# Whole-unit products, other Horner halves and a new step order in a fused attention and rational-activation kernel

## Chip, cores and metric

The kernel runs on one core of a Trainium2 chip. The metric is the device time of one execution in microseconds (us); the time given for a kernel is the median of its runs. An engine name in the text is as the profile has it: PE (TensorE), DVE (VectorE), ACT (ScalarE), POOL (GpSimd), SP (SyncE, which issues most transfers).

## What is computed

A linear attention with squared sketch features, followed by a two-layer network whose activation is a ratio of two polynomials. The core of the reference:

```python
# attention: q, k, v are (4, 4, 1088, 32), S1 and S2 are (8, 32)
def phi(x):
    a = np.einsum('rd,bhsd->bhsr', S1, x)
    b = np.einsum('rd,bhsd->bhsr', S2, x)
    return np.einsum('bhsi,bhsj->bhsij', a, b).reshape(*x.shape[:-1], r * r)
q_p, k_p = (phi(q), phi(k))
kv = np.einsum('bhsf,bhsd->bhfd', k_p, v)
z = np.sum(k_p, axis=2)
num = np.einsum('bhsf,bhfd->bhsd', q_p, kv)
den = np.einsum('bhsf,bhf->bhs', q_p, z)[..., None] + 1e-06
x = (num / den) as (4352, 128)          # tokens by heads * dims

# network: w_in (128, 2048), w_out (2048, 128), a (4,), b (2,)
h = x @ w_in
P = a[0] + a[1] * h + a[2] * h**2 + a[3] * h**3
Q = 1.0 + np.abs(b[0]) * np.abs(h) + np.abs(b[1]) * h**2
out = (P / (Q + 1e-06)) @ w_out
```

## The kernel before

**The order.** Nothing is scheduled by the framework: `ORDER` is a written list of some 700 steps, `name:index`, and the loop at the end of the kernel calls one function for each. The position in the list is the position in the in-order queue of the engine that the step uses. Loads (`lk`, `lq`, `lv` of a batch's K, Q, V; `lw`, `lx` of halves of w_out and w_in; `lq:0` of the rest of the first Q) go to SP's queue, in list order too, together with scratch transfers and stores.

**Attention.** Four batches. For each batch K is transposed on DVE (`kt`), sketched on PE (`ks`), copied on ACT (`kc`), multiplied out on DVE (`kf`), contracted with V on PE (`kp`) and kept by ACT (`kk`). Q goes in blocks of tokens (`:0` to `:12`): transposed (`qt`, DVE), sketched (`qs`, PE), copied (`qc`, ACT; from block 3 on through scratch memory in DRAM, by seven transfers on SP), multiplied (`qf`, DVE), contracted (`qp`, PE), divided (`qd` on ACT or DVE, `qi` and `qx` on DVE), transposed back (`qb`, PE) and copied to `xT` (`qk`, ACT). One SBUF buffer each serves all K and all Q loads, so a load waits for the transposes of the one ahead.

**The network.** The hidden layer is worked in 17 units of 4096 columns each: unit 0 has 256 tokens by all 16 blocks of 128 hidden rows, units 1 to 14 have 512 tokens by 8 blocks, units 15 and 16 have 256 tokens by 16 blocks. In each unit:

- `h0` to `h3` (L455, PE): a part of 1024 columns of h = x @ w_in into one of two PSUM tiles `h_ps`; `e0` to `e3` (L461, ACT) evict it to `hh` in bf16.
- `u` (L484, DVE): |h| by a bit mask; `w` (L490, DVE): |b1| u + |b0|; `y` (L495, DVE): w times u. So w holds Q − 1.
- `ln` (L546) and `ex` (L550, both ACT): r = exp(−ln(1 + 1e-6 + w)) = 1 / Q, always in halves of 2048 columns.
- `p` (`pd` L536 on DVE or `pa` L541 on ACT, by `P_ON_ACT`): a3 h + a2.
- `s` (L554, DVE): s = h r. `m` (L558, DVE): g = h s. `x` (L569, DVE): g = g p. So g = (a3 h + a2) h² r.
- `G0` to `G5` (L588, PE), one group for each half and each of r, s, g: out += r (a0 w_out) + s (a1 w_out) + g w_out, with the two scaled copies of w_out made once (`wo`, L621 to L625). `st` (L597, L605) transposes and stores.

In a **Horner half** (`HORNER` lists 2 × unit + half) m is h p, a step `v` (L564, DVE) adds a1, and x multiplies by s: g = h r (a1 + h (a2 + a3 h)). The s group of that half is then left out on PE.

A step's digit is the half (or quarter in unit 16). `u`, `w`, `y` work on the whole unit at digit 1 unless the unit is in `SPLIT_A`. `s`, `m`, `x`, `p` work in halves unless the unit is in `WIDE_S`, `WIDE_M`, `WIDE_X`, `WIDE_P` and, for m and x, both halves are of one Horner kind or, for p, on one engine; then the step of digit 0 does nothing and that of digit 1 does both halves. (By this rule only s of units 3 and 5 is whole before.) Unit 16 is always in half and quarters.

The buffers behind this: three of `hh`, one of `u`, two of `w`, one of `ln`, and rings of halves: four each of r, s and g, two of p:

```python
rings = {key: big.tile([128, n, HW], BF, name=key) for key, n in (("r", 4), ("s", 4), ("g", 4), ("p", 2))}
```

`tn` (L170) issues matmuls on zeros: `tn:0` eleven, `tn:4` two.

Of the kernel before, what the change touches and what calls it, by code (L numbers as in the profile page):

```python
# [26 lines left out]
ex0:0 u1:1 h2:2 qf:3 w1:1 qc:4 e1:2 qp:3 e2:2 s0:0 pa0:0 h3:2 y1:1 h0:2 qd:3 wo:5 e3:2 qi:3 m0:0 G0:0 e0:2 qx:3 G1:0
ln0:1 kt1:2 x0:0 qb:3 ks0:2 u1:2 qk:3 G2:0 ex0:1 lk:3 pd0:1 G3:0 w1:2 G4:0 pa1:1 kp1:1 y1:2 kc0:2 ln1:1 G5:0 qf:4 lv:2
qs:5 kf0:2 kk:1 ex1:1 qp:4 s0:1 ks1:2 qd:4 qc:5 qi:4 ln0:2 qt:7 G0:1 qx:4 m0:1 qb:4 G1:1 qk:4 s1:1 ex0:2 h3:3 x0:1
kc1:2 h2:3 m1:1 e3:3 kf1:2 h0:3 e2:3 kt1:3 ln1:2 s0:2 h1:3 st:0 m0:2 e0:3 qs:7 x1:1 e1:3 h2:4 ex1:2 u1:3 h3:4 pd1:2  # L30
pa0:2 w1:3 kp1:2 s1:2 e2:4 x0:2 e3:4 h0:4 lv:3 qf:5 pa0:3 y1:3 qp:5 qc:7 e0:4 h1:4 m1:2 qd:5 ln0:3 qi:5 qt:9 G2:1 qx:5
e1:4 x1:2 qb:5 G3:1 qk:5 u1:4 ex0:3 G4:1 m0:3 G5:1 pa1:3 G0:2 w1:4 h0:5 kt0:3 ln1:3 m1:3 h2:5 y1:4 kk:2 ex1:3 ks0:3
G1:2 e0:5 s1:3 G2:2 ln0:4 G3:2 h1:5 v0:3 ex0:4 qf:7 x0:3 G4:2 e2:5 qs:6 s0:4 qc:6 h3:5 e1:5 pd0:4 ln1:4 m0:4 h1:6 v1:3
e3:5 x0:4 pa1:4 h0:6 u1:5 qt:8 G5:2 e1:6 w1:5 ex1:4 h3:6 st:2 y1:5 e0:6 qp:7 e3:6 s1:4 G0:3 pa0:5 lq:3 G2:3 x1:3 qs:8
m1:4 h2:6 ln0:5 m0:5 G3:3 e2:6 x1:4 G5:3 ex0:5 qf:6 G0:4 u1:6 G1:4 qc:8 qd:7 ln1:5 qi:7 qp:6 w1:6 G2:4 qx:7 qd:6 pa0:6
qi:6 v0:5 qb:7 G3:4 qx:6 y1:6 qb:6 qk:7 G4:4 qk:6 ex1:5 h3:7 m0:6 pa1:5 G5:4 s1:5 h1:7 e3:7 st:4 h2:7 m1:5 e1:7 ln0:6
x0:5 h0:7 qt:10 x1:5 e2:7 G0:5 e0:7 qf:8 ks1:3 kc0:3 ex0:6 u1:7 qs:9 h1:8 v0:6 qc:9 w1:7 ln1:6 h3:8 s0:6 e1:8 pd1:6
qp:8 ex1:6 y1:7 h0:8 e3:8 s1:6 kc1:3 ln0:7 h2:8 x0:6 e0:8 m1:6 G2:5 qd:8 ex0:7 G3:5 qi:8 kf0:3 G4:5 kf1:3 G5:5 e2:8
qs:10 ln1:7 u1:8 kp1:3 qx:8 w1:8 ex1:7 qb:8 G0:6 qf:9 qk:8 y1:8 qc:10 h3:9 pa0:7 s0:7 h0:9 e3:9 s1:7 ln0:8 h2:9 qt:12
m0:7 e0:9 G0:7 x1:6 e2:9 h1:10 ex0:8 x0:7 qt:11 h1:9 u1:9 pa0:8 m1:7 G2:6 pd1:7 e1:9 G3:6 s0:8 e1:10 G4:6 u0:9 ln1:8  # L40
h3:10 w1:9 m0:8 qp:9 ex1:8 x1:7 h2:10 x0:8 qd:9 kk:3 e3:10 qi:9 w0:9 pa0:9 h0:10 qf:10 y0:9 qp:10 e2:10 y1:9 e0:10
# [676 lines left out]
```

## Time and profile before

| | |
|---|---|
| runs | 272.06, 272.32 and 272.9 us; median 272.32 |
| profiled execution | span 270.8 us from its first to its last instruction; the median of the runs is 1.5 us above that span |
| ACT | 248.8 us busy, 224 instructions |
| DVE | 256.7 us busy, 278 instructions |
| PE | 257.7 us busy, 1382 matmuls; weight loads 147.5 us |
| granted clock of PE | 0.994 in the mean |
| memory | 16.16 MB read, 3.15 MB written |

How to read the rows: in a timeline row stand start, duration, engine, line, operation, output and inputs, shape, and in brackets the idle time before it with what ended it. In a group row stand the count, busy time and mean duration in ns, then the idle time before its instructions. In a row of stretches stand, for each engine, busy us and the number of instructions. Neighbouring instructions of one engine overlap at their ends, so the step from one start to the next is shorter than the duration.

### The profile page before, as it was taken

The page shows a single profiled execution, that of the slowest core. Times are in us where ns is not written, and L with a number is a line of the kernel's source. Part 1 is how long each engine was busy: PE and PEld are TensorE (multiplying, and loading weights), DVE is VectorE, ACT ScalarE, POOL GpSimd, SP SyncE. Part 2 cuts the span into 40 slices and gives each one's busy share as a digit, 9 for nine tenths or more (in the row PEclk, how much of TensorE's full clock was granted, in tenths as well). Part 3 has the DMA queues.
Part 4 walks back from the last instruction along what each step waited for, and adds up shares of the span by engine and source line. Part 5 has one row for each costly group of instructions (what it writes and reads, how often), then busy time and mean ns, then how long its engine had stood idle before and what let it go on. Part 6 is the DMA issues. An engine that isn't in the chain of part 4 may idle for free.

```text
span 270.8 us, 3732 instructions
## 1 busy us (share of the span) xinstructions
PE 257.7 (95%) x1382; PEld 147.5 (54%) x1397; DVE 256.7 (95%) x278; ACT 248.8 (92%) x224; POOL 2.9 (1%) x24
## 2 busy tenths in 40 slices
...
DMA packets 30530, 19.55 MB, mean 72 GB/s; under 512 B 20400, under 2 KB 26672, under 8 KB 30512
## 3 DMA queue, kind: packets, MB, share of 16 engines
...
q8 instruction: 11, 0.18, 0.3%
...
HBM read 16.16 MB, written 3.15 MB: 71 GB/s over the span
## 4 chain that ended last, share of the span: by engine, by line
ACT 47%; PE 34%; issue 8%; DVE 5%; DMA 4%; SPq 0%; ACTq 0%; DVEq 0%
PE h_ps L455 16%; ACT ln L546 13%; ACT r L550 12%; ACT hh L461 12%; PE att_ps L588 10%; ACT p L541 7%; PE att_ps L365 3%; DMA v_sb<-in_v_dram 2%; PE att_ps L302 2%; DMA k_sb<-in_k_dram 2%; DVE g L558 2%; DVE s L554 1%; ACT xT L398 1%; PE att_ps L391 1%; PE att_ps L409 1%
## 5 line engine op out<-in xcount | busy, mean ns | idle before, releaser
L455 PE MATMUL h_ps<-xT,w_in_sb 128*128 128x512 f32 (+1 forms) x320 | 125.8, 537 | 2.8 <-ACT hh L461 1.9
L455 PEld LDWEIGHTS h_ps<-xT,w_in_sb 128*128 128x128 f32 x320 | 58.3, 190 | 55.2 <-issue 37.3
L461 ACT CAST hh<-h_ps 128x1024 bf16<-128x1024 f32 x68 | 67.5, 1027 | 3.5 <-PE h_ps L455 3.1
L588 PEld LDWEIGHTS <-w_out 128*128 128x128 bf16 x460 | 45.5, 100 | 45.9 <-issue 14.3
L546 ACT ACTIVATE ln<-w 128x2048 f32<-128x2048 bf16 (+1 forms) x35 | 66.0, 1887 | 0.7 <-DVE w L495 0.6
L550 ACT ACTIVATE r<-ln 128x2048 bf16<-128x2048 f32 (+1 forms) x35 | 65.8, 1880 | 0.6 <-PE att_ps L588 0.2
L541 ACT ACTIVATE p<-hh,a_sb 128x2048 bf16<-128x2048 bf16 (+1 forms) x23 | 46.7, 2035 | 0.1
L554 DVE TENSOR_TENSOR s<-hh,r 128x2048 bf16<-128x2048 bf16 (+2 forms) x33 | 41.0, 1246 | 0.2 <-ACT r L550 0.2
L495 DVE TENSOR_TENSOR w<-w,u 128x4096 bf16<-128x4096 bf16 (+2 forms) x22 | 39.4, 1798 | 0.1
L588 PE MATMUL att_ps<-g,w_out 128*128 128x512 bf16 (+1 forms) x154 | 34.8, 350 | 4.3 <-DVE g L569 3.9
L558 DVE TENSOR_TENSOR g<-hh,s 128x2048 bf16<-128x2048 bf16 (+1 forms) x30 | 35.2, 1175 | 0.0
L569 DVE TENSOR_TENSOR g<-g,p 128x2048 bf16<-128x2048 bf16 (+1 forms) x30 | 35.1, 1178 | 0.1
L588 PE MATMUL att_ps<-r,w_out 128*128 128x512 bf16 (+1 forms) x154 | 34.8, 353 | 0.3
L588 PE MATMUL att_ps<-s,w_out 128*128 128x512 bf16 (+1 forms) x137 | 29.3, 342 | 0.2
L490 DVE TENSOR_SCALAR w<-u,b_abs 128x4096 bf16<-128x4096 bf16 (+2 forms) x22 | 23.8, 1090 | 0.0
L484 DVE TENSOR_SCALAR u<-hh 128x4096 uint16<-128x4096 uint16 (+2 forms) x22 | 21.4, 976 | 1.6 <-ACT hh L461 1.5
L365 PEld LDWEIGHTS att_ps<-kvz,q_pT 128*128 128x128 f32 x144 | 17.7, 191 | 4.6 <-issue 2.0
L365 PE MATMUL att_ps<-kvz,q_pT 128*128 128x66 f32 x144 | 17.9, 273 | 0.1
L302 PEld LDWEIGHTS att_ps<-v_sb,k_p 128*64 128x64 f32 (+1 forms) x288 | 8.8, 138 | 1.9 <-DVE qT L325 0.8
L536 DVE TENSOR_SCALAR p<-hh,a_sb 128x2048 bf16<-128x2048 bf16 x12 | 9.7, 808 | 0.0
L302 PE MATMUL att_ps<-v_sb,k_p 128*64 128x64 f32 (+1 forms) x288 | 9.2, 223 | 0.5 <-DMA v_sb<-in_v_dram 0.5
L273 DVE TENSOR_TENSOR k_p<-att_ps,b_sk 128x1024 f32<-128x1024 f32 (+2 forms) x8 | 9.3, 1178 | 0.1
...
## 6 DMA issues: line engine op xcount, KB each, us to landing
...
k_sb<-in_k_dram SPq DMA_DIRECT2D x3, 544.0 KB
q_sb<-in_q_dram SPq DMA_DIRECT2D x3, 544.0 KB
...
w_out_sb_f<-in_moe_w_out_dram SPq DMA_DIRECT2D x2, 512.0 KB
```

The costliest lines, as they stand in the source:

```text
L365: nc.tensor.matmul(self.nd[:, o:o + 2 * KW], lhsT=self.q_p[:, c, x:x + 128], rhs=kvz[self.b % 2][:, c, :], start=True, stop=True)
L455: nc.tensor.matmul(t[:, x * tl:(x + 1) * tl], lhsT=w_in_sb[:, f * 128:(f + 1) * 128], rhs=xT[:, x_at(t0):x_at(t0) + tl], start=True, stop= ...
L461: nc.scalar.copy(out=live[i]["hh"][:, part * PW:(part + 1) * PW], in_=live[i]["h", part])
L490: nc.vector.tensor_scalar(out=t[:, c], in0=live[i]["u"][:, c], scalar1=ab1, scalar2=ab0, op0=AX.mult, op1=AX.add)
L495: nc.vector.tensor_mul(out=t[:, c], in0=t[:, c], in1=live[i]["u"][:, c])
L541: nc.scalar.activation(out=part_of(i, "p", h), in_=hh, func=ACT.Identity, scale=a3, bias=a2)
L546: nc.scalar.activation(out=t, in_=live[i]["w"][:, span(h)], func=ACT.Ln, bias=1.0 + 1e-6)
L550: nc.scalar.activation(out=part_of(i, "r", h), in_=live[i]["ln"], func=ACT.Exp, scale=-1.0)
L554: nc.vector.tensor_mul(out=part_of(i, "s", h), in0=hh, in1=part_of(i, "r", h))
L558: nc.vector.tensor_mul(out=part_of(i, "g", h), in0=hh, in1=part_of(i, "p" if horner(i, first(h)) else "s", h))
L569: nc.vector.tensor_mul(out=g, in0=g, in1=part_of(i, "s" if horner(i, first(h)) else "p", h))
L588: nc.tensor.matmul(outs[t0][:, :tl], lhsT=w_sb[y][:, f0 + x, :], rhs=part_of(i, key, h)[:, c:c + tl], start=done[0] == 0, stop=done[0] == ...
```

## The change

The step list is written anew, and the tables that say which steps are whole are changed. No function changes. After it `s` and `m` are whole in units 1 to 15, `x` in units 0 to 15, `u`, `w` and `y` in units 1 to 15 (before: all but 0, 9, 13 and 16), `p` in units 1, 3 to 9 and 12 to 15, of them 6, 7, 9, 12 and 14 on DVE. As many halves of p are on ACT as before, 22 of 34. The Horner halves are both of unit 0 and both of unit 1. Every line below the tables stands 3 lines earlier in the changed kernel (L554 becomes L551).

```diff
 ORDER = """
-tn:4 tn:0 lw:1 lq:0 kt0:0 lw:0 kt1:0 lx:1 kt2:0 lx:0 ks1:0 kt3:0 ks0:0 lk:1 qt:0 ks2:0 kc0:0 kc1:0 kf0:0 kf1:0 qs:0
-kc2:0 qt:1 kf2:0 qc:0 kp0:0 ba:0 kp1:0 qf:0 kp2:0 wo:3 qs:1 kk:0 lv:1 qt:2 qp:0 qc:1 wo:1 qf:1 qs:2 qd:0 qi:0 qc:2
-qp:1 qx:0 qf:2 wo:0 qb:0 qp:2 qd:1 qi:1 qk:0 qx:1 qt:3 h3:0 qd:2 qi:2 lq:1 qx:2 wo:4 wo:2 h2:0 e3:0 kt1:1 h0:0 kt0:1
-e2:0 pa1:0 u1:0 lk:2 qs:3 w1:0 qb:2 h1:0 y1:0 qc:3 qk:2 e0:0 qt:5 qb:1 ks0:1 qt:4 e1:0 qs:4 qk:1 u0:0 ln1:0 h1:1 qt:6
...
-G2:14 ex1:15 x0:15 G3:14 y0:16 G2:15 v1:14 G3:15 ln0:16 s1:15 x1:14 ex0:16 pd1:15 G5:14 m1:15 G0:16 ln2:16 s0:16 G4:15
-pa0:16 x1:15 G1:16 ex2:16 m0:16 G5:15 ln3:16 s2:16 x0:16 ex3:16 m2:16 G2:16 pa2:16 st:15 s3:16 G3:16 pa3:16 G4:16
-st:14 x2:16 m3:16 G5:16 G6:16 x3:16 G7:16 G8:16 st:16
+lq:0 tn:0 kt0:0 kt1:0 kt2:0 ks1:0 kt3:0 ks0:0 ks2:0 qt:0 kc1:0 kc0:0 qs:0 qt:1 kf0:0 kf1:0 lw:1 kc2:0 kp0:0 kf2:0 qt:2
+lx:1 qc:0 kp1:0 kp2:0 qf:0 qs:1 wo:3 kk:0 qp:0 qd:0 qi:0 qc:1 wo:5 qx:0 qt:3 qs:2 lw:0 qf:1 qb:0 qs:3 lk:1 qk:0 wo:4
+wo:2 ba:0 lq:1 qc:2 h2:0 h3:0 kt1:1 kt0:1 qf:2 qt:5 qt:4 lx:0 qc:3 wo:1 e2:0 wo:0 qp:1 e3:0 qd:1 qi:1 qx:1 pa1:0 qp:2
+h1:0 u1:0 w1:0 qs:4 y1:0 qb:1 m1:0 qd:2 qf:3 qi:2 qx:2 ks0:1 h0:0 qb:2 e1:0 qt:6 lv:1 lk:2 lq:2 qk:1 qc:4 ln1:0 kc0:1
+e0:0 qk:2 pa0:0 v1:0 qs:5 ks1:1 ex1:0 kf0:1 kt1:2 h3:1 e3:1 u0:0 kt0:2 lk:3 qp:3 w0:0 h0:1 kc1:1 h1:1 m0:0 e0:1 y0:0
...
+e2:15 ex0:13 G4:12 s1:13 G0:12 G2:11 pa1:13 h1:15 e3:15 ln0:14 m1:13 h0:15 e1:15 h2:16 e0:15 x1:13 h1:16 G5:12 pd1:14
+ex0:14 e2:16 u1:15 w1:15 y1:15 u2:16 G2:12 st:10 G1:12 ln1:14 w2:16 ex1:14 y2:16 e1:16 s1:14 m1:14 h3:16 h0:16 tn:4
+ln0:15 G0:13 e3:16 e0:16 G3:14 u3:16 G1:13 ex0:15 G3:13 w3:16 u0:16 w0:16 G0:14 G1:14 ln1:15 G4:13 y0:16 G0:15 G5:13
+ex1:15 G2:13 x1:14 s1:15 st:12 G2:14 ln0:16 y3:16 ex0:16 pa1:15 m1:15 G5:14 ln2:16 s0:16 G4:15 G4:14 x1:15 ex2:16
+G0:16 ln3:16 G3:15 ex3:16 pa0:16 pa2:16 m0:16 G1:15 G5:15 s2:16 m2:16 s3:16 G4:16 G3:16 G2:15 pa3:16 G7:16 st:14 x0:16
+m3:16 G1:16 st:15 G6:16 x2:16 x3:16 G2:16 G5:16 G8:16 st:16
 """.split()
-P_ON_ACT = (1, 1, 0, 1, 1, 0, 1, 1, 0, 1, 1, 1, 1, 0, 1, 0, 1, 0, 1, 1, 0, 1, 0, 1, 1, 1, 0, 0, 1, 1, 0, 0, 1, 1)
-SPLIT_A = (0, 9, 13, 16)
+P_ON_ACT = (1, 1, 1, 1, 1, 1, 1, 1, 1, 1, 1, 1, 0, 0, 0, 0, 1, 1, 0, 0, 0, 1, 0, 1, 0, 0, 1, 1, 0, 0, 1, 1, 1, 1)
+SPLIT_A = (0, 16)
 QUARTER = (16,)
 LX = 4
 TAIL = 2
-WIDE_S = (3, 5)
-WIDE_M = (5,)
-WIDE_X = (5, 14)
-WIDE_P = (2,)
-HORNER = (6, 7, 10, 12, 29)
+WIDE_S = (1, 2, 3, 4, 5, 6, 7, 8, 9, 10, 11, 12, 13, 14, 15)
+WIDE_M = (1, 2, 3, 4, 5, 6, 7, 8, 9, 10, 11, 12, 13, 14, 15)
+WIDE_X = (0, 1, 2, 3, 4, 5, 6, 7, 8, 9, 10, 11, 12, 13, 14, 15)
+WIDE_P = (1, 3, 4, 5, 6, 7, 8, 9, 12, 13, 14, 15)
+HORNER = (0, 1, 2, 3)
```

49 lines of the change are left out of this document (21 added, 28 removed).

## Prediction

> **What bounds the kernel now.** I read the page's busy times first, then the stretches of 10 us, then the groups by shape, and last the timelines of the stretches that the change touches.
>
> ```profile
> PE 257.7 (95%) x1382; PEld 147.5 (54%) x1397; DVE 256.7 (95%) x278; ACT 248.8 (92%) x224; POOL 2.9 (1%) x24
> ```
>
> ```profile
> 10.00:20.00 10.00, 9.95 (x125) 8.79 (x126) 7.65 (x18) 5.02 (x14) 0.00 (x0) 1.00 1.06 326
> 120.00:130.00 10.00, 10.00 (x46) 5.89 (x45) 9.94 (x10) 9.90 (x10) 0.00 (x0) 1.00 0.21 38
> 260.00:270.00 10.00, 5.39 (x46) 4.19 (x44) 6.79 (x11) 4.73 (x5) 0.00 (x0) 1.00 0.36 53
> ```
>
> The columns behind the length are PE, PEld, DVE, ACT, POOL, then clock, DMA share, GB/s. Three engines are full at once; in the first 20 us and the last 10 none is. No one stage can be shortened alone: the time is first a sum of work on the fullest engine, DVE, plus what it loses at both ends, and a gain there counts only while ACT and PE hand over in time. DVE starts its first |h| at 22.37 (below) and is busy to 267.6, so DVE's account is the one I make.
>
> **Prices.** Instructions of one engine overlap a little, so I price by the step from one start to the next, not by duration. DVE's timeline (start, duration, instruction):
>
> ```profile
> 22.37 0.69 DVE L484 TENSOR_SCALAR u<-hh 128x2048 uint16<-128x2048 uint16 x1 [0.88 <-ACT hh L461]
> 23.10 0.81 DVE L490 TENSOR_SCALAR w<-u,b_abs 128x2048 bf16<-128x2048 bf16 x1
> 23.95 1.23 DVE L495 TENSOR_TENSOR w<-w,u 128x2048 bf16<-128x2048 bf16 x1
> ...
> 38.65 1.34 DVE L490 TENSOR_SCALAR w<-u,b_abs 128x4096 bf16<-128x4096 bf16 x1
> 39.91 1.22 DVE L554 TENSOR_TENSOR s<-hh,r 128x2048 bf16<-128x2048 bf16 x1
> 41.05 2.28 DVE L495 TENSOR_TENSOR w<-w,u 128x4096 bf16<-128x4096 bf16 x1
> 43.25 0.22 DVE L380 RECIPROCAL rec<-den 128x12 f32<-128x12 f32 x1
> ...
> 249.30 0.81 DVE L490 TENSOR_SCALAR w<-u,b_abs 128x2048 bf16<-128x2048 bf16 x1
> 250.02 1.22 DVE L569 TENSOR_TENSOR g<-g,p 128x2048 bf16<-128x2048 bf16 x1
> ...
> 252.29 0.75 DVE L564 TENSOR_SCALAR g<-g,a_sb 128x2048 bf16<-128x2048 bf16 x1
> 252.95 1.22 DVE L554 TENSOR_TENSOR s<-hh,r 128x2048 bf16<-128x2048 bf16 x1
> 254.09 1.22 DVE L569 TENSOR_TENSOR g<-g,s 128x2048 bf16<-128x2048 bf16 x1
> 255.22 0.81 DVE L536 TENSOR_SCALAR p<-hh,a_sb 128x2048 bf16<-128x2048 bf16 x1
> 255.95 1.22 DVE L558 TENSOR_TENSOR g<-hh,s 128x2048 bf16<-128x2048 bf16 x1
> ```
>
> A half product (s, m, x, y all have this form) steps 254.09 − 252.95 = 1.14 and 255.22 − 254.09 = 1.13; a whole one 43.25 − 41.05 = 2.20. A pair made whole saves 2 × 1.135 − 2.20 = 0.07. Half w is 0.72 (249.30 to 250.02), whole 1.26: 0.18 a pair. Half p is 0.73; a whole p is not in the trace, the whole w is the same form (two per-partition scalars, bf16): 0.20 a pair, bounds 0 and 0.3. Step v is 0.66.
>
> The other price is of order. At 23.10 w is followed by the y that reads it: 0.85, where the w at 249.30, followed by something unrelated, takes 0.72. An instruction that reads the one right ahead of it waits 0.13 more. I take 0.12 for each such neighbour pair.
>
> **The change on DVE.** Counts come from the step lists and these groups:
>
> ```profile
> L554 DVE TENSOR_TENSOR s<-hh,r 128x2048 bf16<-128x2048 bf16 x29 | 35.1, 1213 | 0.0
> L554 DVE TENSOR_TENSOR s<-hh,r 128x4096 bf16<-128x4096 bf16 x2 | 4.6, 2292 | 0.2 <-ACT r L550 0.2
> L536 DVE TENSOR_SCALAR p<-hh,a_sb 128x2048 bf16<-128x2048 bf16 x12 | 9.7, 808 | 0.0
> L541 ACT ACTIVATE p<-hh,a_sb 128x2048 bf16<-128x2048 bf16 x21 | 44.3, 2112 | 0.1
> L546 ACT ACTIVATE ln<-w 128x2048 f32<-128x2048 bf16 x33 | 63.9, 1937 | 0.6 <-DVE w L495 0.6
> ```
>
> - s: whole in 15 units, where 2 were: 13 pairs. m: 15 pairs (none was whole). x: 16 pairs. y: 2 pairs. 46 × 0.07 = −3.2.
> - u and w whole in two more units: 2 × (0.10 + 0.18) = −0.6, u, of which no undisturbed half is shown, put at 0.10 (bounds 0 and 0.18).
> - p stays at 12 halves on DVE, 10 of them now as 5 whole: 5 × 0.20 = −1.0.
> - v: 4 halves instead of 5: −0.7.
> - Order: among u, w, y, s, m, v, x, p the old list has 6 instructions that read the one right ahead, the new one 40 (u, w, y in a row; s, m, x in a row). 34 × 0.12 = +4.1.
>
> Sum −1.4; so nearly all that the wide instructions save is spent on waiting for one another. Bounds: −2.8 with 0.08 a neighbour pair, 0 with 0.16.
>
> By the Trainium skill ("VectorE: DVE Perf Modes", The DRAIN you can't avoid) no Vector instruction starts before the one ahead has emptied the pipe, and a semaphore between two adds nothing. The rows differ on both counts: at 252.95 an instruction of 1.22 gives way after 1.14, and the reader of its neighbour's result starts 0.13 later. By that page no neighbour pair would cost anything; that case is the first rival.
>
> **On ACT and PE.**
>
> ```profile
> 257.32 2.08 ACT L541 ACTIVATE p<-hh,a_sb 128x2048 bf16<-128x2048 bf16 x1
> 259.30 1.04 ACT L550 ACTIVATE r<-ln 128x1024 bf16<-128x1024 f32 x1
> ...
> 262.43 2.36 ACT L541 ACTIVATE p<-hh,a_sb 128x1024 bf16<-128x1024 bf16 x2
> ```
>
> ```profile
> 246.94 1.04 PE L588 MATMUL att_ps<-s,w_out 128*128 128x256 bf16 x8
> 247.82 1.03 PE L588 MATMUL att_ps<-r,w_out 128*128 128x512 bf16 x4
> 248.68 1.03 PE L588 MATMUL att_ps<-s,w_out 128*128 128x512 bf16 x4
> ```
>
> ACT keeps its 21 half p, 14 of them as 7 whole. Half p steps 1.98; two of 1024 end after 2.36, so the first steps some 1.13, and 1024 columns cost 0.85. A whole p is 1.98 + 2 × 0.85 = 3.68, 0.28 less than two: −2.0, bounds 0 and −2.0. PE skips the s product of Horner halves. Before, five halves of 512-token units were skipped, 0.86 each (r, the same form, at 247.82 to 248.68); now two of them and both halves of unit 0, 0.88 each (246.94 to 247.82): +3 × 0.86 − 2 × 0.88 = +0.8 on PE. Neither enters the sum while DVE is last, but they alter the margins: ACT gets air, PE loses it.
>
> **The start.**
>
> ```profile
> 15.13 0.42 DVE L385 TENSOR_TENSOR x_tok<-att_ps,rec 128x256 f32<-128x256 f32 x1
> ...
> 20.12 1.37 DVE L254 STREAM_TRANSPOSE kT<-k_sb 128x224 f32<-128x224 f32 x2 [0.22 <-DMA k_sb<-in_k_dram]
> ```
>
> ```profile
> 17.15 0.37 ACT L398 COPY xT<-att_ps 128x256 f32<-128x256 f32 x1
> ...
> 19.60 1.01 ACT L461 CAST hh<-h_ps 128x1024 bf16<-128x1024 f32 x1 [1.73 <-PE h_ps L455]
> ```
>
> ```profile
> 16.40 0.39 PE L391 MATMUL att_ps<-ident,x_tok 128*128 128x128 f32 x2
> ...
> 17.57 5.45 PE L455 MATMUL h_ps<-xT,w_in_sb 128*128 128x256 f32 x24
> ```
>
> ```profile
> q_sb<-in_q_dram SPq DMA_DIRECT2D x3, 544.0 KB
> w_in_sb<-in_moe_w_in_dram SPq DMA_DIRECT2D x2, 512.0 KB
> ```
>
> x_tok is done at 15.55. Now the transpose stands behind the next block's products on PE, and the copy to xT behind a second w_out scaling on ACT. The new order puts the transpose ahead of those products and the copy ahead of that scaling: transpose near 15.6, copy near 16.0, hidden layer near 16.4 (block 3's sketches in between), 1.2 earlier. One part takes 5.45 / 3 = 1.8, so the second is done near 20.0; but two w_out scalings now stand around its eviction on ACT, which ends near 21.2 where it ended at 22.3. That is −1.1 for ACT. DVE has more to do ahead of its first u: both transposes of batch 1's K, block 2's features, two transposes of batch 1's Q, block 1's division. On SP's queue K 1 now passes one w_in half and V 1 goes far back; at the 326 GB/s of the stretch from 10 us, 512 KB less is 1.6 us: K lands near 18.5 instead of 20.1, Q behind it near 20.2 (544 KB, 1.7; its load also waits until block 3's transposition has emptied the one buffer, near 16). Block 3's scratch transfers now stand behind both on SP, and DVE wants them only after the first y. Q's transposes and the division end near 22.0, and u starts there: −0.4 against 22.37, bounds −1.1 (the eviction alone decides) and +0.6 (Q a microsecond later). w_in's first half is last on the queue, near 21.9, and its hidden part stands behind the products of blocks 1 and 2 on PE, near 22: just covered.
>
> **The tail.**
>
> ```profile
> 265.75 0.69 DVE L569 TENSOR_TENSOR g<-g,p 128x1024 bf16<-128x1024 bf16 x1
> ...
> 267.13 0.45 DVE L597 STREAM_TRANSPOSE out_sb<-att_ps 128x256 f32<-128x256 f32 x1 [0.69 <-PE att_ps L588]
> ```
>
> DVE works without a gap until 266.4, then the last four matmuls and the last store follow. The new list ends with the same x3, G8, st. It moves unit 16's first p behind the last exp on ACT (2.0 + 2.36 = 4.3 to ACT's end), but DVE then has s, a store, x0, m, a store and x2 to do: 0.6 + 0.6 + 1.1 + 0.6 + 0.4 + 0.6 = 3.9 before x3. 0, bounds −0.5 and +0.5. The two idle matmuls moved in there (0.4) lie in PE's free time (5.39 of 10 us busy).
>
> **Sum.** −1.4 − 0.4 + 0 = −1.8 on a span of 270.8: 269.0. The median of the runs, 272.3, lies 1.5 above the span, so 270.5.
>
> **Rivals.**
>
> *Faster still.* A whole instruction saves its full difference in duration (2 × 1.213 − 2.292 = 0.134 by the groups) and neighbours cost nothing. Then DVE would lose some 46 × 0.134 + 2.3 = 8.5, and ACT would be last: −2.0 of p, −1.1 at the start, its 0.6 of waits for w: −3.7, 268.6. The steps above speak against it.
>
> *No change: PE sets the pace.* Ahead of the last hidden part of unit 13 the lists have on PE 56 hidden and 63 output parts before, 56 and 60 after (−3 × 0.86 = −2.6). Ahead of its eviction ACT has one ln fewer (−1.9), one half p fewer and five pairs whole (−2.0 − 1.4): −5.3. So PE's lead over ACT shrinks by 2.7. Where ACT waits for PE, DVE's 1.8 is not realised; with PE's +0.8 and a start at −0.4 the time is 272.7. For it: PE is as full as DVE in every stretch. Against it: DVE keeps a lead of its own, since it waits for whole units that ACT delivers earlier.
>
> *Slower: the p buffer.* It holds one unit. A whole p on ACT (7 units) can start only when the whole x of the unit ahead has ended, 1.07 later than a half x would; evictions, logarithms and so PE are queued behind it on ACT. Decisive once DVE runs later than ACT's turn for p. At worst 7 × 1.07 = 7.5; with half of it, +3.7 − 1.8: 274.2. For it: unit after unit the new list puts p close behind that x. Against it: ACT waited 0.1 in all ahead of p (L541), and it gains 3.1 elsewhere. The Trainium skill ("Perfetto Trace Analysis", Optimizing Scalar/DVE Operations) says that grouping pays on a saturated engine and that smaller instructions finish sooner where another engine starves; no row here decides which holds.
>
> That the wide forms do not come about is excluded by the instruction lists.
>
> **Chances.** Forecast 0.44 (its own range 269.4 to 271.6: bounds of order price and start), faster still 0.10, no change 0.22, slower 0.24. Below 0.3% (0.8 us) a measurement here can't tell a difference. Faster: 0.42 + 0.10; same: 0.02 + 0.19; slower: 0.24 + 0.03. The range 268.2 to 273.9 leaves out the worse half of the slower case and the edge of the fast one.
>
> **What would show it.** Right: DVE's instructions fall from 278 to near 220 while its busy time falls by no more than about 5; steps of a u-w-y row 0.1 above those of lone ones; the first u near 22.0; DVE without gaps to its last x. Wrong: ACT waiting ahead of p for x (L538 after, the p buffer); evictions waiting for hidden matmuls by microseconds in 150 to 220 (PE's pace); whole products stepping well under 2.2, or neighbours at no extra.

## The result, and the profile after

| | before | after |
|---|---|---|
| runs | 272.06 to 272.9 us, median 272.34 | 284.28 to 286.82 us, median 285.52 |
| ratio | | 1.0476, 95% interval 1.0449 to 1.0504 |
| profiled span | 270.8 us | 285.0 us |
| DVE busy; span less DVE busy | 256.7; 14.1 us | 254.2; 30.8 us |
| waits of DVE for the scratch transfers | none | 14.2 us in 5 |

Slower by 13 us, where 270.5 was forecast and the range ended at 273.9. The ratios here and below leave out executions in which the chip ran disturbed. The profiled execution of the changed kernel was the longest of its four (spans 282.5 to 285.0 us), and that of several runs below was their shortest, so a difference of spans overstates what a run gained on it; where the two differ, the ratio counts.

The page of the changed kernel, busy times and the chain that ended last by engine:

```profile
PE 264.5 (93%) x1393; PEld 150.7 (53%) x1393; DVE 254.2 (89%) x222; ACT 247.6 (87%) x217; POOL 2.9 (1%) x24
...
DVE 53%; DMA 17%; issue 9%; ACT 9%; PE 7%; SPq 3%; DVEq 0%; ACTq 0%
```

DVE's instructions fell to 222 and its work by 2.5 us, as the forecast had it. But DMA holds 17% of the chain that sets the end. The waits, longest sums first (us in total, times, longest):

```profile
DVE q_pT L429 <- DMA b_all<-sk_d: 14.2, 5, 4.3
ACT ln L543 <- DVE w L492: 7.8, 6, 3.6
```

DVE's loss grew by 30.8 − 14.1 = 16.7, and 14.2 of that is one kind of wait: the feature step `qf` of a block stands on DVE before its operand b_all has come back from scratch memory. Blocks 3, 4 and 7 make 12.4 of the 14.2. ACT then waits for the w that stands behind. DVE's timeline:

```profile
21.82 0.68 DVE L481 TENSOR_SCALAR u<-hh 128x2048 uint16<-128x2048 uint16 x1
22.55 0.81 DVE L487 TENSOR_SCALAR w<-u,b_abs 128x2048 bf16<-128x2048 bf16 x1
23.39 1.23 DVE L492 TENSOR_TENSOR w<-w,u 128x2048 bf16<-128x2048 bf16 x1
24.53 1.22 DVE L555 TENSOR_TENSOR g<-hh,p 128x2048 bf16<-128x2048 bf16 x1
30.03 0.82 DVE L429 TENSOR_TENSOR q_pT<-a_all,b_all 128x640 f32<-128x640 f32 x1 [4.28 <-DMA b_all<-sk_d]
...
71.20 0.96 DVE L429 TENSOR_TENSOR q_pT<-a_all,b_all 128x768 f32<-128x768 f32 x1 [4.24 <-DMA b_all<-sk_d]
```

The start came as forecast: first u at 21.82 (22.0). Then, right behind y and m, block 3's features stand still for 4.28. Where the transfer was shows SP's queue (start, us spent issuing, transfer), with ACT's copy of block 4 below it:

```profile
15.41 0.33 SPq L121 DMA_DIRECT2D q_sb<-in_q_dram  x1
15.79 0.76 SPq L651 DMA_DIRECT2D w_in_sb<-in_moe_w_in_dram  x1
16.86 1.73 SPq L417 DMA_DIRECT2D sk_d<-sk_sb  x4
22.39 0.54 SPq L420 DMA_DIRECT2D a_all<-sk_d  x1
22.98 1.33 SPq L423 DMA_DIRECT2D b_all<-sk_d  x2
...
31.94 0.35 SPq L121 DMA_DIRECT2D q_sb<-in_q_dram  x1
32.38 2.58 SPq L417 DMA_DIRECT2D sk_d<-sk_sb  x4
```

```profile
24.79 0.34 ACT L412 COPY sk_sb<-att_ps 128x192 f32<-128x192 f32 x1
```

The read into a_all is issued 5.5 us after the writes to sk_d, behind a Q load and half of w_in; the last read ends its issue at 24.3 and lands 5.7 later. Block 4 shows a second loss: its copy was done at 25.1, but its writes go out at 32.38. Ahead of them in the queue stands batch 2's Q load (31.94), which waits for the last transpose of batch 1's Q, and on DVE that stood behind the first wait. The same in the kernel before, with the features of that block:

```profile
24.67 1.73 SPq L420 DMA_DIRECT2D sk_d<-sk_sb  x4
27.66 0.54 SPq L423 DMA_DIRECT2D a_all<-sk_d  x1
28.25 1.32 SPq L426 DMA_DIRECT2D b_all<-sk_d  x2
```

```profile
37.92 0.81 DVE L432 TENSOR_TENSOR q_pT<-a_all,b_all 128x640 f32<-128x640 f32 x1
```

There 3.0 us lie between writes and read, and DVE asks for the features 8.4 us after the last issue ended. The stretches of the changed kernel (columns as in the prediction):

```profile
30.00:40.00 10.00, 8.36 (x33) 5.62 (x34) 8.90 (x13) 5.37 (x5) 0.00 (x0) 0.66 0.58 156
40.00:50.00 10.00, 10.00 (x98) 5.96 (x97) 6.12 (x9) 8.37 (x11) 0.00 (x0) 1.00 0.44 110
100.00:110.00 10.00, 9.64 (x39) 4.47 (x38) 10.00 (x9) 10.00 (x10) 0.00 (x0) 1.00 0.02 6
270.00:280.00 10.00, 7.18 (x52) 5.68 (x52) 8.96 (x11) 6.96 (x6) 0.00 (x0) 0.83 0.25 38
280.00:290.00 10.00, 0.68 (x7) 0.36 (x4) 0.45 (x1) 0.00 (x0) 0.00 (x0) 0.83 0.12 18
```

From 90 us on DVE is all but as full as before (157.9 of the 160 us up to 250, 159.4 before); the loss lies between 20 and 90, where DVE is idle for 15.6 us instead of 2.5.

The forecast's prices, on DVE and ACT of the changed kernel:

```profile
111.11 1.34 DVE L487 TENSOR_SCALAR w<-u,b_abs 128x4096 bf16<-128x4096 bf16 x1
112.37 2.28 DVE L566 TENSOR_TENSOR g<-g,p 128x4096 bf16<-128x4096 bf16 x1
114.57 1.22 DVE L270 TENSOR_TENSOR k_p<-att_ps,b_sk 128x1024 f32<-128x1024 f32 x1
...
125.25 1.35 DVE L487 TENSOR_SCALAR w<-u,b_abs 128x4096 bf16<-128x4096 bf16 x1
126.63 2.29 DVE L492 TENSOR_TENSOR w<-w,u 128x4096 bf16<-128x4096 bf16 x1
...
132.26 2.25 DVE L551 TENSOR_TENSOR s<-hh,r 128x4096 bf16<-128x4096 bf16 x1
134.62 2.29 DVE L555 TENSOR_TENSOR g<-hh,s 128x4096 bf16<-128x4096 bf16 x1
```

```profile
48.81 3.80 ACT L538 ACTIVATE p<-hh,a_sb 128x4096 bf16<-128x4096 bf16 x1
52.52 0.17 ACT L373 ACTIVATE den<-att_ps 128x12 f32<-128x12 f32 x1
```

A whole product steps 2.20 (112.37 to 114.57), a whole w 1.26 and 0.12 more ahead of its own y (125.25 to 126.63), a whole p on ACT 3.71: 2.20, 1.26, 0.12 and 3.68 had been taken. Between s and the m that reads it the price is higher: m starts 0.11 after the end of s, and the step is 2.36, 0.16 over 2.20 (132.26 to 134.62).

### The profile page after: what moved, and what is told of

Its sections match the earlier page's. It is cut to its first block, busy times and chain, and to the rows that moved or that the text cites. A ratio compares the mean times of both kernels' runs of the same rounds, so it can differ in the third digit from the quotient of the medians.

```text
span 285.0 us, 3663 instructions
## 1 busy us (share of the span) xinstructions
PE 264.5 (93%) x1393; PEld 150.7 (53%) x1393; DVE 254.2 (89%) x222; ACT 247.6 (87%) x217; POOL 2.9 (1%) x24
## 4 chain that ended last, share of the span: by engine, by line
DVE 53%; DMA 17%; issue 9%; ACT 9%; PE 7%; SPq 3%; DVEq 0%; ACTq 0%
DVE g L555 11%; DMA b_all<-sk_d 10%; DVE s L551 10%; DVE g L566 8%; DVE w L492 5%; DVE w L487 5%; DVE u L481 4%; ACT ln L543 3%; ACT r L547 3%; DMA v_sb<-in_v_dram 3%; DMA sk_d<-sk_sb 3%; PE att_ps L585 2%; DVE p L533 2%; ACT hh L458 2%; DVE q_pT L429 2%
## 5 line engine op out<-in xcount | busy, mean ns | idle before, releaser
L452 PE MATMUL h_ps<-xT,w_in_sb 128*128 128x512 f32 (+1 forms) x320 | 129.3, 539 | 2.5 <-ACT hh L458 2.3
L538 ACT ACTIVATE p<-hh,a_sb 128x2048 bf16<-128x2048 bf16 (+2 forms) x16 | 43.7, 2741 | 0.0
L551 DVE TENSOR_TENSOR s<-hh,r 128x4096 bf16<-128x4096 bf16 (+2 forms) x20 | 39.2, 1958 | 0.0
L555 DVE TENSOR_TENSOR g<-hh,s 128x4096 bf16<-128x4096 bf16 (+2 forms) x17 | 34.6, 2034 | 0.7
L566 DVE TENSOR_TENSOR g<-g,p 128x4096 bf16<-128x4096 bf16 (+2 forms) x17 | 34.4, 2031 | 0.6
L585 PE MATMUL att_ps<-s,w_out 128*128 128x512 bf16 (+1 forms) x136 | 30.6, 358 | 1.0 <-DVE s L551 1.0
L429 DVE TENSOR_TENSOR q_pT<-a_all,b_all 128x768 f32<-128x768 f32 (+1 forms) x10 | 9.0, 897 | 14.3 <-DMA b_all<-sk_d 14.2
L299 PE MATMUL att_ps<-v_sb,k_p 128*64 128x64 f32 (+1 forms) x288 | 10.6, 241 | 2.6 <-DVE k_p L270 2.6
L299 PEld LDWEIGHTS att_ps<-v_sb,k_p 128*64 128x64 f32 (+1 forms) x288 | 10.1, 155 | 4.6 <-DVE k_p L270 3.4
L388 PE MATMUL att_ps<-ident,x_tok 128*128 128x128 f32 x36 | 6.4, 287 | 5.4 <-DVE x_tok L382 4.6
```

Source lines behind the costliest of these rows:

```text
L452: nc.tensor.matmul(t[:, x * tl:(x + 1) * tl], lhsT=w_in_sb[:, f * 128:(f + 1) * 128], rhs=xT[:, x_at(t0):x_at(t0) + tl], start=True, stop= ...
L538: nc.scalar.activation(out=part_of(i, "p", h), in_=hh, func=ACT.Identity, scale=a3, bias=a2)
L551: nc.vector.tensor_mul(out=part_of(i, "s", h), in0=hh, in1=part_of(i, "r", h))
L555: nc.vector.tensor_mul(out=part_of(i, "g", h), in0=hh, in1=part_of(i, "p" if horner(i, first(h)) else "s", h))
L566: nc.vector.tensor_mul(out=g, in0=g, in1=part_of(i, "s" if horner(i, first(h)) else "p", h))
L585: nc.tensor.matmul(outs[t0][:, :tl], lhsT=w_sb[y][:, f0 + x, :], rhs=part_of(i, key, h)[:, c:c + tl], start=done[0] == 0, stop=done[0] == ...
```

## The experiments

Theory A: the new list asks for transferred data sooner after its issue than the transfers take, and DVE, which works in list order, stands still. Rivals: the whole forms hand over too late; one edit of the list alone; the new order of the network's steps. All runs, with the ratio to the kernel before, the profiled span, DVE's busy time, and DVE's waits for scratch and for K, all in us. Scratch is what the profile puts down to b_all's transfer; ahead of the features another 0.9 us in x2, 0.7 in x3, 1.3 in x8 and 0.5 in x13 is put down to the writes to scratch, and 1.4 in x3 to nothing that the profile shows.

| run | ratio [95%] | span | DVE busy | scratch | K |
|---|---|---|---|---|---|
| kernel before | 1 | 270.8 | 256.7 | none | 1.7 |
| changed kernel | 1.048 [1.045, 1.050] | 285.0 | 254.2 | 14.2 | 1.1 |
| x1_const | 1.026 [1.022, 1.031] | 276.7 | 254.1 | none | 5.8 |
| x1_const_before | 1.000 [0.999, 1.001] | 270.9 | 256.5 | none | 2.1 |
| x2_lq | 1.046 [1.041, 1.052] | 282.4 | 254.3 | 10.5 | 2.5 |
| x3_qf | 1.045 [1.042, 1.047] | 282.2 | 254.0 | 7.9 | 3.8 |
| x5_noload | 1.009 [1.005, 1.013] | 272.4 | 254.2 | none | 2.2 |
| x6_halves | 1.017 [1.011, 1.023] | 274.6 | 259.2 | none | 1.7 |
| x7_halves_full | 1.057 [1.052, 1.062] | 284.6 | 259.4 | 10.6 | 1.3 |
| x8_poolq | 1.056 [1.053, 1.060] | 286.4 | 254.4 | 8.8 | 2.1 |
| x9_early_before | 1.083 [1.080, 1.087] | 292.7 | 256.9 | 17.3 | 3.0 |
| x10_fix | 1.049 [1.046, 1.052] | 283.1 | 254.6 | 7.5 | 2.7 |
| x11_wide_before | 1.144 [1.141, 1.147] | 309.2 | 256.4 | none | 2.9 |
| x12_pick | 1.040 [1.038, 1.041] | 282.8 | 256.7 | none | 2.7 |
| x13_ab2 | 1.044 [1.042, 1.046] | 283.0 | 253.9 | 11.8 | 3.3 |
| x14_ab2_early | 1.043 [1.041, 1.045] | 282.3 | 254.2 | 4.0 | 2.1 |
| x15_spread | 1.191 [1.189, 1.193] | 320.8 | 255.3 | none | 3.1 |

**Features without their transfers (x1).** The features of blocks 3 to 12 read columns of w_in instead of a_all and b_all, in the changed kernel and, as a control, in the kernel before. The transfers are still issued; the kernel leaves out the true features.

```diff
-            nc.vector.tensor_mul(..., in0=self.a[:, :2 * self.n]..., in1=self.bb[:, :2 * self.n]...)
+            nc.vector.tensor_mul(..., in0=w_in_sb[:, 0:2 * self.n]..., in1=w_in_sb[:, 1024:1024 + 2 * self.n]...)
```

> The changed kernel with one thing left out: the feature product of blocks 3 to 12 (qf) reads two slices of w_in instead of the two tiles that come back from scratch memory, so the output is not the reference's. The transfers are still issued, in the same places; only DVE's wait for their landing is gone. Theory A (DVE stands still in its queue for the scratch round trip, 14.2 us in 5 waits, and nothing else is wrong): 285.5 - 14.2 = 271.3, near the 270.5 forecast, and DVE idle between 20 and 90 us falls from 15.6 to under 3. Rival B (whole units make the hand-over between ACT, DVE and PE too coarse, and the waits for scratch only lie where the other waits would be): the time stays above 278, and waits of ACT for w, or of DVE for r or hh, grow in place of those for scratch. Rival C (part of both): 273 to 278.

> The kernel before with the same thing left out, as a control: qf of blocks 3 to 12 reads slices of w_in instead of the scratch tiles; the transfers stay; the output is not the reference's. Before, DVE never waited for scratch. A, B and C alike: 272.3 within 0.5. A fall of more than 1 us would mean that reading other tiles is itself a gain, which then is to be taken off the first run.

The control did not move. In the changed kernel the scratch waits went and the span fell by 8.3, but the ratio gives back only 5.8 of the 13 us: about 279.8, not the 271.3 of theory A. That lies in the range of rival B, whose mechanism isn't there: ACT's waits for w fell from 7.8 to 5.9, and the wait that came up is again one for a transfer:

```profile
DVE kT L251 <- DMA k_sb<-in_k_dram: 5.8, 2, 4.4
```

With the scratch waits gone DVE reaches the transposes of the next K before K is there. The new list is tight at more than one transfer.

**One edit of the list at a time (x2, x3).**

```diff
-... qt:6 lv:1 lk:2 lq:2 qk:1 qc:4 ln1:0 ...
+... qt:6 lv:1 lk:2 qk:1 qc:4 lq:2 ln1:0 ...
```

```diff
-... m1:0 qd:2 qf:3 qi:2 qx:2 ks0:1 h0:0 qb:2 e1:0 qt:6 lv:1 ...
+... m1:0 qd:2 qi:2 qx:2 ks0:1 h0:0 qb:2 e1:0 qt:6 qf:3 lv:1 ...
```

> The changed kernel with one load moved in the list: the load of batch 2's Q goes behind block 4's scratch transfers on SP's queue (it waits for a transpose on DVE that itself stands behind the first wait for scratch; the transfers of block 4 were issued at 32.4 for this). Everything is computed. A: the second wait (3.88 us) falls to under 0.5, the others stay: 281 to 282.5. If SP's blocking is not the cause of the second wait: 285 to 286.

> The changed kernel with one step moved in the list: block 3's features (qf) go behind the division of block 2 and the next transpose of Q on DVE, some 1.2 us of work that needs no scratch. Everything is computed. A: the first wait falls from 4.28 to near 3, PE and ACT no longer stand still for the division (4.6 and 4.2 us there), Q's load gets out early so that the second wait also shrinks: 279.5 to 283. B: 284 to 286.

They took 3.7 and 6.3 us off the waits for b_all, some of which came back under other names (see above the table); the intervals of the ratio overlap the changed kernel's: the gain expected did not come. K's wait grew (1.1 to 2.5 and 3.8). In x2 block 4's writes did leave earlier, at 26.98 instead of 32.38, but its read into a_all was issued only 7.1 us after them instead of 5.1, with V and K loads issued just ahead, and the wait fell to 1.50, not to under 0.5.

**Almost no late data (x5).** As x1, and besides, the transposes of K and Q in batches 2 and 3 read w_in. All transfers are still issued, and none of them waits any longer for those transposes to empty its buffer; the kernel leaves out the true features, and K and Q of the last two batches.

```diff
-            k_in = self.k_sb.rearrange(
+            k_in = (self.k_sb if self.b < 2 else w_in_sb[:, 0:NM * W]).rearrange(
-            ... in_=self.q_sb[:, self.c0:self.c0 + self.n])
+            ... in_=(self.q_sb if self.b < 2 else w_in_sb)[:, self.c0:self.c0 + self.n])
```

> The changed kernel with DVE freed of every late transfer after the start: as in x1_const the features of blocks 3 to 12 read slices of w_in, and the transposes of K and Q of batches 2 and 3 read w_in too. All transfers are still issued in their places; the output is not the reference's. In x1_const 5.8 us of waits for K came up in place of the 14.2 for scratch, and its profiled span of 276.7 lies 5.9 above the 270.8 of before. Theory A (the new list puts the steps that read transfers closer behind their issue than the transfers take; the rest of the change is worth what was forecast): span 269 to 271.5, median 270.5 to 273. Rival B (whole units make the hand-over coarse): the span stays at 275 or more, with waits between engines in place of those for transfers.

```profile
PE 258.6 (95%) x1393; PEld 146.8 (54%) x1393; DVE 254.2 (93%) x222; ACT 247.4 (91%) x217; POOL 2.9 (1%) x24
```

The ratio falls from 1.048 to 1.009: of the 13.0 us that the change had added, some 10.6 are gone (in the profiled spans 12.6 of 14.2), with list, whole forms, Horner halves and every transfer in place. So DVE's dependence on late data is most of the loss, and the new order of the network's steps is not. Theory A had this at 270.5 to 273 and is missed by some 2 us: the time is near 275, and the profiled span stays 1.6 above the one before.

**Whole or half (x6, x7).** x5, and the changed kernel itself, with s, m, x, u, w, y of units 1 to 15 and x of unit 0 as two halves side by side where the whole one stood. x6 leaves out what x5 does.

```diff
-SPLIT_A = (0, 16)
+SPLIT_A = tuple(range(17))
-WIDE_S = (1, 2, ...
+WIDE_S = ()
...
-... u1:3 w1:3 ...
+... u0:3 u1:3 w0:3 w1:3 ...
```

> x5_noload with s, m, x, u, w and y of units 1 to 15 as two half instructions at the place of the whole one; p as it was, transfers left unread as in x5_noload. By the account of the prediction: s, m, x, y 61 pairs x 0.07 = +4.3, u and w 15 x 0.28 = +4.2, and about 37 neighbour pairs no longer read the instruction right ahead, -4.4: +4.1 on x5_noload. If neighbours cost nothing: +8.5. If a whole instruction saved its full difference in duration and neighbours cost nothing: +14. If coarse hand-over is what costs (B): faster than x5_noload.

> The changed kernel with all its transfers read, and s, m, x, u, w and y of units 1 to 15 as two halves at the place of the whole one; everything is computed. A: DVE still waits for scratch, 12 to 15 us, and the time is 285 to 290. B: falls towards 278 or less.

```profile
PE 259.7 (95%) x1393; PEld 147.1 (54%) x1393; DVE 259.2 (94%) x313; ACT 247.8 (90%) x217; POOL 2.9 (1%) x24
```

The line is x6's. With 91 more instructions DVE has 5.0 more work and the span is 2.2 longer, half of the 4.1 expected; the intervals of x5 and x6 overlap. With everything computed (x7) halves bring nothing back either: the time is 0.9% above the changed kernel's. So in the new list the whole forms are worth some 2 us, and no cost of their coarse hand-over shows, as far as halves side by side can show it.

**Loads on another queue (x8).** K, Q and V loads of the later batches, and V of the first, are issued by POOL, so that they block no scratch transfer.

```diff
-        nc.sync.dma_start(out=t, in_=q[b]...)
+        nc.gpsimd.dma_start(out=t, in_=q[b]...)
```

> The changed kernel with the loads of K, Q and V of batches 0 (V) and 1 to 3 issued from POOL's queue instead of SP's; scratch transfers and stores stay on SP; everything is computed. Tells apart two parts of theory A. If the loads and scratch transfers hold each other up because SP issues them in one order and each waits for its own buffer: block 4's scratch transfers are issued by 31 instead of 37.4, the second wait and those for K go, 277 to 281. If the transfers are simply asked for too late: 283 to 287. The start may lose a microsecond where POOL issues V of batch 0 more slowly.

```profile
PE 263.9 (92%) x1393; PEld 150.2 (52%) x1393; DVE 254.4 (89%) x222; ACT 247.6 (86%) x217; POOL 17.7 (6%) x46
```

The waits for b_all fell to 8.8 and block 4's is gone (its writes leave at 29.12 instead of 32.38), but POOL is busy 17.7 instead of 2.9 us, and the ratio is 1.056, which is neither of the two cases expected. The start lost 4.8 us: the first u stands at 26.59 instead of 21.82. As the time rose by 2.4 only, the rest got some 2.4 shorter: an estimate by which the loads on SP's queue are a part of the loss.

**The loss made in the kernel before (x9).** Nothing but five feature steps is moved ahead:

```diff
-... h2:1 kf0:1 ks1:1 ... G1:0 ln0:1 kt1:2 ... m1:1 e3:3 kf1:2 ... qf:3 ... qf:4 ... qf:5 ...
+... h2:1 qf:3 kf0:1 ks1:1 ... G1:0 ln0:1 qf:4 kt1:2 ... m1:1 e3:3 qf:5 kf1:2 ...
```

> The kernel before, with nothing of the change in it but one thing: five feature steps (blocks 3, 4, 5, 7 and 6) are moved ahead in the list by 4 to 10 us of DVE's work. On its timeline they would start near 29.8, 44.9, 61.1, 79.3 and 97.0, that is 5 us after the last copy of their block (24.7, 38.5, 55.7, 74.3, 92.1), where now 13 us or more lie between. In the kernel before the scratch transfers' last issue ends 4.9 us after the copy, and the broadcast read lands some 4 us after its issue, so the features are there 9 us after the copy. Theory A (the distance from the copy to the features in the list sets the loss): DVE waits 3 to 4 us for b_all in each of the five, 15 to 18 in all, and as DVE has next to no slack the time rises by 10 to 17: 282 to 289, a ratio of 1.037 to 1.062. Rival B (the waits in the changed kernel only take up time that DVE would lose anyway to ACT and PE in the new order): waits appear, but the time rises by less than 5, under 277. Rival C (transfers are late in the changed kernel because of its loads and its packed queue alone): the features are there in time here, no wait above 1 us, ratio within 0.01 of 1.

DVE's timeline, the last read of block 3 on SP's queue, and the sums of the waits:

```profile
33.94 0.83 DVE L432 TENSOR_TENSOR q_pT<-a_all,b_all 128x640 f32<-128x640 f32 x1 [4.55 <-DMA b_all<-sk_d]
...
71.57 0.96 DVE L432 TENSOR_TENSOR q_pT<-a_all,b_all 128x768 f32<-128x768 f32 x1 [3.85 <-DMA b_all<-sk_d]
```

```profile
27.71 1.32 SPq L426 DMA_DIRECT2D b_all<-sk_d  x2
```

```profile
DVE q_pT L432 <- DMA b_all<-sk_d: 17.3, 4, 5.0
ACT ln L546 <- DVE w L495: 10.4, 4, 4.7
```

Block 3's data is there 4.9 us after its last read was issued (29.03 to 33.94). The sum of the waits is as foretold, 15 to 18, but in four of the five features: block 4's didn't wait, the others waited 3.9 to 5.0. The span rises by 21.9 for 17.3 of them, and the time by 8.3%, more than foretold: what stands behind them on DVE makes ACT wait too. With no whole form, no Horner half and no load moved, the place of the features alone makes a loss larger than that of the change.

**Trying to undo it by order (x10).** In the changed kernel `qf` of blocks 3, 4, 5, 7, 6, 8 and the transposes of batch 2's K are moved later, `lv:1` and `lq:2` behind K's load. The copies of blocks 4, 5, 6 and 8 move later too, behind the features of the block ahead, with which they share a buffer. So `lq:2` still stands ahead of block 4's copy, other than the expectation says.

```diff
-... qd:2 qf:3 qi:2 ... kf0:1 kt1:2 h3:1 e3:1 u0:0 kt0:2 lk:3 qp:3 w0:0 ... kf1:1 qf:4 ... u1:1 qx:3 ex0:0 ... w1:1 ...
+... qd:2 qi:2 ... kf0:1 qf:3 qc:4 h3:1 e3:1 u0:0 qp:3 w0:0 kt1:2 kt0:2 lk:3 ... kf1:1 ... u1:1 qx:3 ex0:0 ... w1:1 qf:4 ...
```

> The changed kernel, all computed, with the steps that read transfers put later: features of blocks 3, 4, 5, 7, 6 and 8 by 4 to 8 us of DVE's work, the transposes of batch 2's K behind the second half of unit 0's first steps, batch 1's V and Q loads behind K's load and behind block 4's scratch transfers. Theory A: the scratch waits fall from 14.2 us to under 5, and the time falls towards the 275.7 of the kernel without late transfers: 275 to 280. Rival B (the new order as a whole is too tight: what is gained at the features comes back as waits of ACT and PE for later features): waits for scratch fall as well, but the time stays above 281, and ACT's waits for DVE grow by what the scratch waits lost.

```profile
71.52 1.23 DVE L481 TENSOR_SCALAR u<-hh 128x4096 uint16<-128x4096 uint16 x1 [2.60 <-ACT hh L458]
...
87.27 0.96 DVE L429 TENSOR_TENSOR q_pT<-a_all,b_all 128x768 f32<-128x768 f32 x1 [5.10 <-DMA b_all<-sk_d]
```

The rival's case by the numbers: the scratch waits halved, the time did not fall. But the edit lengthens the way from copy to features in some blocks only: block 4's writes leave at 32.72, no sooner than before (32.38), and block 8's features now wait 5.10 (87.27) where they had waited 0.31. DVE also waits for evictions of a later hidden part (71.52).

**Two buffers, and earlier copies (x13, x14).** a_all and b_all get two buffers each (the room comes from the tile of zeros); in x14 the copies are moved ahead as well.

```diff
-    PB, AB = 1, 1
+    PB, AB = 1, 2
-    idle = consts.tile([128, 512], BF, name="idle")
+    idle = consts.tile([128, 320], BF, name="idle")
```

```diff
-... qs:4 y1:0 ... qs:5 ks1:1 ... qs:7 qc:7 lv:2 ... qf:7 qc:6 ...
+... qs:4 qc:4 y1:0 ... qs:5 qc:5 ks1:1 ... qs:7 qc:7 qc:6 lv:2 ... qf:7 qc:8 ...
```

> The changed kernel with two buffers each for a_all and b_all instead of one, its list unchanged; the room comes from the tile of zeros for the idle matmuls (320 columns instead of 512, and 18 and 3 matmuls instead of 11 and 2). All is computed. Theory A (the places in the list set the loss): the list still puts each block's copy behind the features of the block ahead, so little changes: scratch waits 10 to 14, time 283 to 287. Rival (the single buffer holds the transfers up): reads into a_all start as soon as the scratch is written, scratch waits under 6, time under 280.

> The same with two buffers, and the copies (and with them the scratch transfers) of blocks 4, 5, 6 and 8 moved ahead in the list to where their sketches or buffers are ready, by 1 to 20 places, and batch 2's K load ahead of block 4's transfers. The features stand where the changed kernel has them, and all is computed. Theory A: the distance from copy to features grows by 4 to 10 us in blocks 4, 5, 6 and 8; block 3's wait (4.3) and block 7's (4.2) stay for the most part; scratch waits 5 to 9 instead of 14.2, time 277 to 282. Rival B (the loss is the new order's as a whole, the scratch waits only show it): the scratch waits fall as well, but ACT and PE take up the time and it stays at 284 or above.

The waits of x14:

```profile
DVE q_pT L429 <- DMA b_all<-sk_d: 4.0, 3, 3.0
ACT sk_sb L412 <- DMA sk_d<-sk_sb: 3.9, 2, 3.0
...
DVE qT L322 <- DMA q_sb<-in_q_dram: 3.5, 3, 2.7
```

The buffer alone did little, as theory A had it. With the copies moved the scratch waits fell by 10.2, more than expected, and still the time fell by little more than 1 us (ratio 1.043 for 1.048) and is where the rival had it: now ACT waits for the one copy buffer and DVE for Q. That goes against theory A in its narrow form; with x1 it suggests that the scratch round trip is the first of a row of transfers that are all asked for too soon.

**Whole forms in the old list (x11, x12).** x11 makes 37 pairs of s, m and x whole in the kernel before; x12 only seven, and u, w, y of units 9 and 13 and p of 13. In both the steps that would then read or overwrite too early are moved in the list as well, in x11 many of them p.

```diff
-WIDE_S = (3, 5)
+WIDE_S = (1, 2, 3, 4, 5, 6, 7, 8, 9, 10, 11, 12, 13, 14, 15)
...
```

```diff
-SPLIT_A = (0, 9, 13, 16)
+SPLIT_A = (0, 16)
-WIDE_X = (5, 14)
+WIDE_X = (3, 10, 12)
...
```

> The kernel before with its own list, and s whole in units 1 to 15, m and x whole in the same units but 5, 6 and 14 (whose two halves are of different Horner kinds): 37 pairs more than before. A whole product stands where the second half stood; only what would read or overwrite too early is moved back (the p of units 3, 5, 8, 9 and 12 on ACT by 9 to 35 places, two output groups of unit 15 by 14). The account of the prediction: 37 x 0.07 = 2.6 saved, 10 more neighbour pairs at 0.12 = 1.2 lost, so -1.4: 270.9, ratio 0.993 to 0.998. Rival (a whole product hands over too late: p stands behind whole products, the output groups of the first halves come later): ACT waits for DVE ahead of p (L541) by some microseconds, and the time is 274 to 278. Either way no wait for b_all above 1 us, since the features stand where they stood: had whole units anything to do with the loss of the changed kernel, it would show here as a ratio near 1.05.

> The kernel before with its own list and whole instructions only where they cost no new neighbour and move nothing far: u, w, y of units 9 and 13, p of unit 13, s of 7 and 13, m of 10 and 12, x of 3, 10 and 12. By the account: u and w 2 x 0.28, y 2 x 0.07, p 0.20, 7 pairs x 0.07 = 0.49, less 3 neighbour pairs x 0.12: -1.0, so 271.3, ratio 0.994 to 0.998. Rival: the first half of u in units 9 and 13 comes 4 to 9 places later, ln waits for w and the time does not fall (ratio 0.999 to 1.006).

Both expectations failed, x11 by +39, x12 by +11 us, without any wait for scratch. In x12, on PE and on ACT:

```profile
105.11 1.86 PE L588 MATMUL att_ps<-g,w_out 128*128 128x512 bf16 x4 [2.15 <-DVE g L569]
```

```profile
110.15 1.01 ACT L461 CAST hh<-h_ps 128x1024 bf16<-128x1024 f32 x1 [3.96 <-PE h_ps L455]
```

The output group of unit 3's first half now needs the whole x. It stands on PE where the half was done in time, PE waits 2.15, the hidden matmuls behind it come late, and ACT waits 3.96. That is one place; over the whole of x12 ACT waits 9.1 us for hidden matmuls, 3.1 in the kernel before. The same in x11, where ACT, DVE and PE wait for each other in turn:

```profile
DVE u L484 <- ACT hh L461: 21.7, 10, 3.9
ACT hh L461 <- PE h_ps L455: 21.0, 15, 7.0
...
ACT p L541 <- DVE g L569: 12.6, 4, 4.8
```

So the coarse hand-over does cost, 11 and 39 us, in a list that was laid for halves; in the list laid for whole units no such cost shows (x6, x7). The Trainium skill ("Perfetto Trace Analysis", Optimizing Scalar/DVE Operations) says that grouping can pay on a saturated engine, and that smaller instructions may help where Scalar or Vector isn't saturated but makes another engine wait. Here DVE was 95% busy, and grouping cost time all the same in the old list: the busy share alone did not decide it.

**The attention at its old spacing (x15).** The network's steps in the new order and form, all attention steps and loads at the share of the network's work at which the old list has them.

```diff
-... v0:0 e2:1 qi:3 u1:1 qx:3 ex0:0 kk:1 kc0:2 ks1:2 qp:4 qb:3 w1:1 s0:0 y1:1 pa1:1 kf0:2 qd:4 e0:2 ...
+... v0:0 qd:3 wo:5 e2:1 qi:3 u1:1 ex0:0 qx:3 w1:1 s0:0 kt1:2 y1:1 qb:3 ks0:2 qk:3 pa1:1 e0:2 ...
```

> The changed kernel, all computed, with its tables and with the network's steps in its own new order; the attention's steps, all loads and the copies of w_out stand between them at the share of the network's work at which the list before has them (a little earlier where a hidden part needs its block sooner; two steps of block 8 up to 15 places later, where a PSUM bank comes free). The features of blocks 3 to 12 so stand at 6 to 71% of the network's work, as before (7 to 72%), where the changed kernel has them at 2 to 50%. Theory A, in its wider form (the attention is laid denser than its transfers can follow): no wait for b_all above 1 us and under 3 in all, waits for K and Q under 3, and the time falls to 270 to 277. Rival B (the new order of the network's steps, or the whole forms, cost the time): the transfer waits go as well, but ACT and PE wait instead, and the time stays at 281 or above.

```profile
DVE rec L377 <- ACT den L373: 21.1, 7, 6.8
DVE u L481 <- ACT hh L458: 18.0, 8, 3.6
ACT xT L395 <- PE att_ps L388: 15.9, 8, 4.1
```

No wait for b_all is left, but a list mixed by a rule of proportion sets the steps of a block's division so close that the engines wait for each other. It separates nothing: the rival's number came out for another reason.

## Why the prediction was wrong, point by point

- **The step that failed** is in the prediction's start: "Block 3's scratch transfers now stand behind both on SP, and DVE wants them only after the first y." It named the wait and gave it no price, for that block nor for the others; the sum was "work on the fullest engine, DVE, plus what it loses at both ends", with no term for data that comes late in between. The rows of before had half of the price: 4.9 us from the first write to the end of the last read's issue (24.67 to 29.57); landing takes 4.9 more (x9). After the change the writes begin at 16.86 and the first y and m end at 25.8, 8.9 later: short by 0.9 already, without the Q load and w_in ahead of them in the queue, and b_all is there at 30.0. Five such waits make 14.2. In x9 such waits of 17.3 cost 21.9; without late data 10.6 of the 13.0 are gone (x5).
- **DVE's account** had the right terms, but the neighbours cost more than it took. −5.5 for fewer instructions and +4.1 for neighbours were forecast. Busy time fell by 2.5. Against that, the gaps of under 0.12 us between DVE's instructions (its timelines from 22 us on) grew from 0.4 us in 11 to 2.6 in 46: 0.03 to 0.04 each in u, w, y (126.63 follows an end at 126.60), mostly 0.10 to 0.11 between s and m, or m and x (134.62 follows one at 134.51). So the account comes to −0.4 where −1.4 was forecast: inside its bounds, −2.8 to 0, near their end. Why s, m, x cost more stays open. On the rule of the Trainium skill ("VectorE: DVE Perf Modes", The DRAIN you can't avoid): the section adds that a next instruction that isn't held starts earlier, which the prediction left out, and the rows agree, as an independent successor starts 0.08 before the end (112.37). A successor that reads the result starts 0.03 to 0.11 after it, where the section counts nothing for a semaphore in between.
- **ACT's p** (3.71 for 3.68) and **the start** (21.82 for 22.0) held. **The tail** didn't: DVE is busy for 8.96 + 0.45 of the last 15.0 us, so it loses 5.6 where it lost 270.8 − 260 − 6.79 = 4.0; +1.6 against 0 ± 0.5. The prediction says: "The new list ends with the same x3, G8, st." It doesn't: of the output groups of unit 16, G2 and G5 now stand behind the last x too. 16 matmuls of 1.91 us follow on PE from 278.76, where one group of 4 (0.60) had to, and DVE waits 1.72 for its last transpose instead of 0.69. That is 1.0 of the 1.6; what follows that transpose is longer by the rest.
- **The rivals.** *Faster still* fell with the neighbour price. *PE's pace* and *the p buffer* did not decide: ACT's waits for hidden matmuls are 4.3 us, all before 42, and its idle time ahead of p (L538) is 0.0 in the group rows of after. The sign of the slower side was given 0.27, its mechanism was another.
- **What the runs settle.** The same list, forms and transfers without late data: ratio 1.009 (x5). The old list with early features: 1.083 (x9). Both point the same way, and halves for whole units take nothing off (x6, x7: 0.8 and 0.9% slower).
- **What stays open.** No version that computes everything and keeps the new list lost less than 1.043. Lengthening one distance uncovered the next (K in x1, ACT's copy buffer and Q in x14, hidden parts in x10), which fits an attention laid too dense for its transfers as a whole; x15, meant to show that, did not. And x5 stays above the kernel before by 0.9%, some 2.4 us, where −1.8 was forecast. In the profiled spans, 1.6 above, the miss of 3.4 is found in DVE's rows: 1.0 in the neighbours, some 0.7 in the tail, and 1.6 in small waits for evictions, copies and products between 22 us and the tail (3.3 in six, 1.7 in four before); no run tries these. In the changed kernel PE's granted clock was low after PE had stood still (last section); what that cost beside the waits, no run separates. None of the runs beat the kernel before.
